# Induced attention and an ELU feed-forward layer on one core: the first batch's product of h and w_in written in place, and a new order of the work

## The chip, the cores and the metric

The kernel runs on one core of a Trainium2 chip. The metric is the device time of one execution in microseconds (us). A core has five engines that run side by side, each through its own list of instructions in order: TensorE (PE, matmuls), VectorE (DVE), ScalarE (ACT), GpSimd (POOL) and SyncE (SP), which here issues all the transfers. They wait for one another by semaphores only. PE writes to PSUM, which DVE and ACT read and POOL cannot.

## What is computed

The reference, cut to what matters (B = 4, N = 12480, C = 128, m = 32 inducing rows, d_ff = 2048):

```python
def mab(q, kv):
    s = scale * (q @ kv.transpose(0, 2, 1))
    s = s - s.max(-1, keepdims=True)
    a = np.exp(s)
    a /= a.sum(-1, keepdims=True) + 1e-09
    return a @ kv
h = mab(I, x)              # [B, 32, 128]
x = mab(x, h)              # [B, N, 128]
h = x @ w_in               # [B*N, 2048]
g = np.where(h > 0.0, h, alpha * (np.exp(np.minimum(h, 0.0)) - 1.0))
return (g @ w_out).astype(np.float32)
```

The weights w_in and w_out come as float64, the rest as float32.

## The kernel before

**Work.** Each batch of 12480 rows is cut into 25 blocks of 512 or 480 rows, in seven groups of 4, 4, 4, 3, 4, 4 and 2 blocks. A batch goes through two halves. The first half gives h of the batch: per group, scores against the inducing rows (`scores`, L443; PE tile ps_s, then a copy s on ACT and a row maximum pm on DVE), a common bias from the maxima so far (`bias_of`, L466), exp on ACT and a transpose eT on DVE (`weights_of`, L502), and the weighted sum of x (`gather`, L515; PE tile ps_hh). At the end the sums es are added up (`sum_es`, L547), h is normalised (`norm_h`) and transposed four times side by side into hT4 (`spread_h`, L583, tile hT). The second half is the attention of x to h (`attend`, L630; scores ps_t, softmax on DVE, ACT and POOL, tiles s2, mx, sm and aT) and the two layers.

**Product of h and w_in.** Instead of the attention output times w_in the kernel multiplies the 32 attention weights of a row by the 32 x 2048 product h @ w_in. Both factors are split into a high and a low float32r part, so layer one is a product of a stack of 96 rows (high, high, low of the attention weights, the tiles stk, and rows of 1/32 below) with a stack hw of 96 rows (high, low, high of the product, and rows of 1 below). `project_h` (L593) makes hw: four matmuls beside one another, each 32 rows wide, put a quarter of the product into each quarter of the partitions of one PSUM tile ps_hw; ACT copies the high part, DVE subtracts to get the low part, and 12 transfers of 64 KB move the pieces to their rows and columns of hw (L620).

**Layers.** A unit (`unit`, L722) is 256 of the 2048 columns for one block: two layer-one matmuls into a PSUM buffer ph (three of these), exp on ACT (e), a max/min step on DVE, the split of the result into gh and gl, and layer-two matmuls into po (L796). Eight units make a block. The plan "PDPDPDPN" says for each which engine makes gl: POOL (P, L765 and L769), DVE (D, L760), or none, with a slower fp32 matmul instead (N).

**First batch.** Its x arrives in row layout (tiles xm), is transposed by PE (ps_x, L866) and copied to xT by DVE and ACT in turn (L875). For the other batches x arrives a second time as xq and DVE transposes it (L419). The first half of batch 1 is spread over the units of batch 0. The first block of batch 0 has an attention of its own (`attend` with lone), all on DVE and ACT, which writes its stk directly.

**Weights.** Each 512-column piece of a float64 weight goes through `weight_steps` (L355): nine steps on DVE, ACT and POOL that put the double together as a float32. There are four pieces of w_in and four of w_out; w_out is then split into wo_h (ACT, L918) and wo_l (POOL, L921), 128 columns at a time.

**Order.** All instructions are first collected as operations with an engine, a key, an estimated duration and what they read and write. `Program.order` (L134) then simulates them: on each engine it takes, of the operations that could start at the earliest time or within LOOK ns of it, the one with the smallest key. It assumes a wake-up time for an operation that waits for another engine (WAKE), a hold of 60 ns for each transfer on SP, a half-speed PE up to 40 us (WARM), and gives out two PSUM banks for all that isn't ph: ps_s, ps_hh, ps_t, ps_hw and po share them. The result is one fixed list per engine. Buffers of one tag are reused in program order. All durations in it are the planner's own estimates.

Of the kernel before, what the change touches and what calls it, by code (L numbers as in the profile page):

```python
# [17 lines left out]
P = 128  # L18
Q = 32
# [59 lines left out]
class Program:  # L79
# [167 lines left out]
def pe(n, passes=1):  # L247
    return passes * n / 2.4 + (17 if passes == 1 else 5), 165.0
# [3 lines left out]
def kernel(  # L252
# [102 lines left out]
    def weight_steps(raw, lo, key, dst, last):  # L355
        part = new([P, WS], U32, "o", "w_part")
        n = WS

        def words():
# [29 lines left out]
        add("DVE", key, dve(n)[0], lambda: nc.vector.scalar_tensor_tensor(  # L389
            out=words()[0].bitcast(F32), in0=words()[1], scalar=2.0**-20,  # L390
            in1=words()[0].bitcast(F32), op0=ALU.mult, op1=ALU.add,
        ), r=[H, L], w=[L], lag=108)
# [4 lines left out]
    def load_raw(t, src, key):  # L397
        add("SP", key, 60.0, src, w=[(t, "d")], nbytes=4 * math.prod(t.shape))
# [8 lines left out]
    def load_xT(b, h, key):  # L407
# [5 lines left out]
        for dq in range(4):  # L413
            add("SP", key, 60.0, lambda dq=dq: nc.sync.dma_start(
                xq()[dq * Q : (dq + 1) * Q],
                src[:, dq * Q : (dq + 1) * Q].rearrange("(u t) d -> t u d", t=Q),
            ), r=[("w_out",)], w=[(xq, dq)], nbytes=n * Q * 4 * 2)
# [24 lines left out]
    def scores(b, g, key):  # L442
# [15 lines left out]
        add("ACT", key, act(T, True)[0], lambda: nc.scalar.copy(  # L458
# [32 lines left out]
    def load_xm(b, g, v, key, tag="xm"):  # L491
# [10 lines left out]
    def weights_of(b, g, i, key):  # L502
# [8 lines left out]
        add("DVE", key, dve(T, True)[0], lambda: nc.vector.transpose(e()[:np_], s()[:np_]),  # L511
# [3 lines left out]
    def gather(b, g, key, first, scale):  # L515
# [17 lines left out]
        if first:  # L533
            h = st["h"] = new([P, C], F32, "h", f"h_{b}")
            add("DVE", key, dve(C)[0], lambda: nc.vector.tensor_copy(h(), ps()[:, :C]),
                r=[(ps, 0)], w=[(h, 0)], lag=108)
        elif scale is not None:
            h = st["h"]
            add("DVE", key, dve(C)[0], lambda: nc.vector.scalar_tensor_tensor(
                out=h(), in0=h(), scalar=scale(), in1=ps()[:, :C], op0=ALU.mult, op1=ALU.add  # L540
            ), r=[(ps, 0), (h, 0), (scale, 0)], w=[(h, 0)], lag=108)
# [51 lines left out]
    def project_h(b, key):  # L593
# [23 lines left out]
        for c in range(4):  # L617
            for i in range(3):
                part = (hw_h, hw_l)[i % 2]
                add("SP", key, 60.0, lambda c=c, i=i, part=part: nc.sync.dma_start(  # L620
                    hw()[i * Q : (i + 1) * Q, c * n : (c + 1) * n].bitcast(F32),
                    part()[c * Q : (c + 1) * Q, :].bitcast(F32),
                ), r=[(part, 0)], w=[(hw, c, i)], nbytes=Q * n * 4)

# [97 lines left out]
    def unit(b, k, cp):  # L722
# [19 lines left out]
        add("PE", n, 2 * pe(T)[0], layer_one,  # L742
# [3 lines left out]
        add("ACT", n, act(2 * T, True)[0], lambda: nc.scalar.activation(  # L746
# [3 lines left out]
        add("DVE", n + KMID, dve(2 * T)[0], lambda: nc.vector.scalar_tensor_tensor(  # L750
            out=ga(), in0=ph()[:, :, :T], scalar=1.0, in1=e(), op0=ALU.max, op1=ALU.min
        ), r=[(ph, 0), (e, 0)], w=[(g, 0)], lag=108)
        if how != "N":
            gh = new(shape, F32R, "gh", f"gh_{n}")
            add("ACT", n + KGH[how], act(2 * T, how == "D")[0], lambda: nc.scalar.activation(  # L755
# [3 lines left out]
        if how == "D":  # L759
            add("DVE", n + KGL, dve(2 * T)[0], lambda: nc.vector.scalar_tensor_tensor(  # L760
# [3 lines left out]
        else:  # L764
            add("POOL", n + KMID, pool_one(2 * T)[0], lambda: nc.gpsimd.tensor_scalar(  # L765
                out=e(), in0=e(), scalar1=-1.0, scalar2=1.0, op0=ALU.add, op1=ALU.mult
            ), r=[(e, 0)], w=[(e, 0)], lag=45)
        if how == "P":
            add("POOL", n + KMID, pool_two(2 * T)[0], lambda: nc.gpsimd.tensor_sub(  # L769
# [18 lines left out]
        for m, piece in enumerate(pieces):  # L788
# [14 lines left out]
            add("PE", n + KOUT, len(piece) * one, layer_two,  # L803
                r=reads + [("wo", 2 * cp), ("wo", 2 * cp + 1)], w=[(po, cp, m)], lag=165)
        if cp == NCP - 1:
            o = new([P, U, Q], F32, "o", f"o_{b}_{k}")
# [5 lines left out]
            for dq in range(4):  # L812
                add("SP", n + KOUT, 60.0, lambda dq=dq: nc.sync.dma_start(
# [202 lines left out]
```

## Time and profile before

| | |
|---|---|
| time, median of 3 runs | 1746.35 us (1746.22 to 1750.83) |
| profiled execution | 1745.76 us, of it the span from first to last instruction 1744.0 us |
| mean granted PE clock | 0.981 of full |
| moved by DMA | 98.18 MB, mean 56 GB/s |
| DVE / ACT / POOL busy | 1530.7 / 1487.9 / 1564.5 us |

All times inside the profile count from the first instruction. A busy time of an engine is the sum of its instructions; matmuls overlap, and their durations contain the pipeline. "Idle before" is the time an engine stood before an instruction, and the arrow names what ended it. L is a line of the kernel; SPq is the queue of transfers on SP. In the tables a group of instructions is one line with the count behind x, the busy time in us and the mean in ns. In the list by time the first column is the start in us, the second the length. The granted clock is the share of PE's pulses that the chip let through in a stretch.

### The profile page before, as it was taken

How to read it: one execution, taken by the hardware profiler on the slowest of the kernel's cores; microseconds unless marked ns; L12 is line 12 of the kernel's file. 1: busy time of each engine (PE TensorE's matmuls, PEld its weight loads, DVE VectorE, ACT ScalarE, POOL GpSimd, SP SyncE). 2: the span in 40 equal slices, each digit the busy share in tenths (PEclk: the TensorE clock that was granted, in tenths of full speed). 3: DMA queues.
4: the chain of work that ended last, by engine and by line, in shares of the span. 5: the costliest groups of instructions: out<-in, count | busy, mean ns of one | idle time of the engine just before them, and what ended most of it. 6: DMA issues, size and time to landing. Idle time of an engine off the chain costs nothing.

```text
span 1744.0 us, 23334 instructions
## 1 busy us (share of the span) xinstructions
PE 1667.7 (96%) x7652; PEld 1198.6 (69%) x7652; DVE 1530.7 (88%) x1610; ACT 1487.9 (85%) x1710; POOL 1564.5 (90%) x1041
## 2 busy tenths in 40 slices
PE   5679999999999999999999999999999999999998
PEld 3357766767766776677766776667776777777776
DVE  5789889898899989988899989998889989888886
ACT  5479989888888988888988988889888889989986
POOL 3479999999898999799999999989999999999998
PEclk8689999999999999999999999999999999999999
DMA  8341232232333233222144223112112111111111
GB/s 268 68 73 40 52 80 57 52 83 51 74 73 66 55 71 73 56 64 52 40 78 71 51 57 68 26 45 52 38 36 45 26 31 29 26 31 31 27 18 18
DMA packets 384762, 98.18 MB, mean 56 GB/s; under 512 B 364864, under 2 KB 370784, under 8 KB 384384
## 3 DMA queue, kind: packets, MB, share of 16 engines
q1 hardware_dynamic: 384640, 96.68, 26.0%
q8 instruction: 61, 1.00, 0.2%
q14 instruction: 61, 0.50, 0.1%
HBM read 48.94 MB, written 25.56 MB: 43 GB/s over the span
## 4 chain that ended last, share of the span: by engine, by line
PE 63%; POOL 13%; DVE 11%; issue 6%; ACT 5%; DMA 2%; SPq 0%; POOLq 0%; DVEq 0%; ACTq 0%
PE po L796 45%; PE ph L736 15%; POOL gl L769 7%; POOL e L765 4%; DVE e L750 3%; ACT e L746 2%; DVE gl L760 2%; DVE ph L750 2%; ACT gh L755 2%; PE ps_t_False L645 1%; PE ps_s L451 1%; POOL alo L705 1%; PE ps_hh L523 1%; DVE apart L471 1%; DVE sm_False L679 1%
## 5 line engine op out<-in xcount | busy, mean ns | idle before, releaser
L769 POOL TENSOR_TENSOR gl<-e,gh 128x1024 fp32r<-128x1024 f32 (+1 forms) x400 | 940.0, 2351 | 19.5
L746 ACT ACTIVATE e<-ph 128x1024 f32<-128x1024 f32 (+1 forms) x800 | 782.9, 1007 | 121.1 <-PE ph L736 112.6
L750 DVE SCALAR_TENSOR_TENSOR e<-ph,e 128x1024 f32<-128x1024 f32 (+1 forms) x500 | 590.8, 1187 | 122.9 <-ACT e L746 118.6
L765 POOL TENSOR_SCALAR e<-e 128x1024 f32<-128x1024 f32 (+1 forms) x500 | 511.9, 1031 | 100.2 <-ACT gh L755 87.0
L796 PE MATMUL po<-gh,wo_h 128*128 128x512 f32 (+1 forms) x1400 | 557.1, 398 | 3.7 <-DVE o L807 2.0
L796 PE MATMUL po<-gh,wo_l 128*128 128x512 f32 (+1 forms) x1400 | 546.1, 390 | 0.0
L736 PE MATMUL ph<-stk,hw 128*128 128x512 f32 (+1 forms) x1600 | 488.9, 405 | 25.2 <-DVE e L750 16.3
L755 ACT ACTIVATE gh<-e 128x1024 fp32r<-128x1024 f32 (+1 forms) x400 | 417.9, 1045 | 39.1 <-DVE e L750 35.9
L796 PE MATMUL po<-gl,wo_h 128*128 128x512 f32 (+1 forms) x1400 | 444.0, 410 | 5.9 <-POOL gl L769 5.6
L736 PEld LDWEIGHTS ph<-stk,hw 128*128 128x128 f32 x1600 | 292.6, 189 | 143.1 <-DVE e L750 33.4
L760 DVE SCALAR_TENSOR_TENSOR gl<-ph,gh 128x1024 fp32r<-128x1024 f32 (+1 forms) x300 | 356.3, 1188 | 35.3 <-ACT gh L755 34.4
L750 DVE SCALAR_TENSOR_TENSOR ph<-ph,e 128x1024 f32<-128x1024 f32 (+1 forms) x300 | 357.0, 1190 | 3.3 <-ACT e L746 2.9
L796 PEld LDWEIGHTS po<-gl,wo_h 128*128 128x128 f32 x1400 | 253.4, 188 | 118.4 <-POOL gl L769 55.3
L755 ACT ACTIVATE gh<-ph 128x1024 fp32r<-128x1024 f32 (+1 forms) x300 | 301.5, 1005 | 31.8 <-DVE ph L750 20.7
L796 PEld LDWEIGHTS po<-gh,wo_h 128*128 128x128 f32 x1400 | 263.7, 188 | 85.8 <-ACT gh L755 14.7
L796 PEld LDWEIGHTS po<-gh,wo_l 128*128 128x128 f32 x1400 | 263.6, 188 | 54.1 <-issue 3.3
L796 PE MATMUL po<-e,wo_n 128*128 128x512 f32 (+1 forms) x400 | 187.5, 591 | 0.5 <-POOL e L765 0.5
L796 PEld LDWEIGHTS po<-e,wo_n 128*128 128x128 f32 x400 | 75.7, 192 | 58.6 <-issue 48.6
L807 DVE STREAM_TRANSPOSE o<-po 128x512 f32<-128x512 f32 (+1 forms) x100 | 69.2, 692 | 11.5 <-PE po L796 11.2
L419 DVE STREAM_TRANSPOSE xT<-xq 128x1024 f32<-128x1024 f32 (+2 forms) x39 | 45.0, 1155 | 5.2 <-DMA xq<-in_x_dram 5.0
L451 PE MATMUL ps_s<-xT,indT 128*32 128x512 f32 (+1 forms) x200 | 33.0, 642 | 16.8 <-DVE xT L875 10.7
L669 POOL TENSOR_TENSOR s_False<-s_False,mx_False 128x512 f32<-128x512 f32 (+3 forms) x28 | 28.9, 1032 | 15.3 <-DVE mx_False L666 15.3
(98 smaller groups left out, 572.4 us busy)
## 6 DMA issues: line engine op xcount, KB each, us to landing
xm<-in_x_dram SPq DMA_DIRECT2D x32, 512.0 KB, 4.5
out_dram<-o SPq DMA_DIRECT2D x240, 64.0 KB, 1.9
xq<-in_x_dram SPq DMA_DIRECT2D x84, 128.0 KB, 3.0
out_dram<-o SPq DMA_DIRECT2D x160, 60.0 KB, 1.9
stk<-ahi SPq DMA_DIRECT2D x118, 64.0 KB, 2.0
xq<-in_x_dram SPq DMA_DIRECT2D x60, 120.0 KB, 2.9
stk<-ahi SPq DMA_DIRECT2D x80, 60.0 KB, 2.0
stk<-alo SPq DMA_DIRECT2D x59, 64.0 KB, 2.0
```

The costliest lines, as they stand in the source:

```text
L419: add("DVE", key + 4.0, dve(n, True)[0], lambda: nc.vector.transpose(t(), xq().rearrange("p u d -> p (u d)")), r=[(xq, dq) for dq in range ...
L451: nc.tensor.matmul(ps()[j * Q : (j + 1) * Q, :T], indT, block_xT(b, g0 + j), start=True, stop=True)
L669: add(on, at(), two[0], lambda: eng.tensor_tensor(out=s(), in0=s(), in1=mx()[:np_].unsqueeze(2).broadcast_to([np_, U, Q]), op=ALU.subtract ...
L736: nc.tensor.matmul(ph()[:, j, :T], st["hw"]()[:, f * P : (f + 1) * P], homes[i][:, :T], start=True, stop=True,)
L746: add("ACT", n, act(2 * T, True)[0], lambda: nc.scalar.activation(e(), ph()[:, :, :T], AF.Exp, bias=-1.0), r=[(ph, 0)], w=[(e, 0)], lag=118)
L750: add("DVE", n + KMID, dve(2 * T)[0], lambda: nc.vector.scalar_tensor_tensor(out=ga(), in0=ph()[:, :, :T], scalar=1.0, in1=e(), op0=ALU.ma ...
L755: add("ACT", n + KGH[how], act(2 * T, how == "D")[0], lambda: nc.scalar.activation(gh(), ga(), AF.Copy, bias=-1.0), r=[(g, 0)], w=[(gh, 0) ...
L760: add("DVE", n + KGL, dve(2 * T)[0], lambda: nc.vector.scalar_tensor_tensor(out=gl(), in0=ga(), scalar=-1.0, in1=gh().bitcast(F32), op0=AL ...
L765: add("POOL", n + KMID, pool_one(2 * T)[0], lambda: nc.gpsimd.tensor_scalar(out=e(), in0=e(), scalar1=-1.0, scalar2=1.0, op0=ALU.add, op1= ...
L769: add("POOL", n + KMID, pool_two(2 * T)[0], lambda: nc.gpsimd.tensor_sub(gl(), e(), gh().bitcast(F32)), r=[(e, 0), (gh, 0)], w=[(gl, 0)], ...
L796: nc.tensor.matmul(po()[:, :T], w(), g_(), start=po.count == 0, stop=po.count == po.total - 1)
L807: add("DVE", n + KOUT - 1, dve(T, True)[0], lambda: nc.vector.transpose(o().rearrange("p u d -> p (u d)"), po()[:, :T]), r=po.parts, w=[(o ...
```

## The change

It has four parts.

1. A new `project_first` makes hw of batch 0 (the other batches keep `project_h`). hT4 holds h four times side by side, so one matmul with all of it gives the product in all four quarters of the partitions: for each quarter of the columns one full-width fp32 matmul into a ph buffer, an ACT copy of 96 rows into hw, and a DVE subtraction that replaces rows 32 to 63 by the low part. No transfer is left in it. The transfers of batch 1 (xq) wait until the last PE operation of `project_first` has run.
2. Batch 0 uses two softmax phases (groups 0 to 2 and 3 to 6) instead of five.
3. w_out is split in steps of up to 512 columns instead of 128: three whole quarters, and a quarter in two pieces of 256. One piece of w_in and one of w_out (WALT) do one DVE step on ACT and POOL instead. The temporary of w_out's pieces uses the buffers of xq instead of those of o.
4. The planner's estimates, look-aheads and all keys are new: a transfer holds SP for 590 ns, PE's wake-up is 200 ns and 60 more for who waits for PE, no slow start of PE, and each kind of operation has its own key offset. In the first stage the attention chain of batch 0 has smaller keys than all steps of the weights.

The core of the diff:

```diff
-WARM = 40000.0
-KMID, KGL, KOUT = 1.0, 1.6, 5.0
-KGH = {"D": 1.5, "P": 2.0}
-KATT = (-37.6, 2.2)
-KWIN, KWOUT, KWSTEP = -1000.0, -20.0, 4.0
-LOADS = (-1009.0, -1008.0, -1007.0, -1006.0)
+WARM = 0.0
+ISSUE = 590.0
+LOOK0 = 0.0
+KATT = (-44.1, 3.68)
-LOOKS = {"PE": 0.0, "ACT": 60.0, "DVE": 60.0, "POOL": 0.0, "SP": 0.0}
+LOOKS = {'PE': 191, 'ACT': 149, 'DVE': 243, 'POOL': 0.0, 'SP': 0.0}
+
+K = {'inP': 0.28, 'inD': -1.6, 'inN': -2.15, 'expP': 1.04, 'expD': 0.24, 'expN': 1.15, 'midP': 1.28, 'midD': 0.66, 'midN': -1.32, 'ghP': 2.33, 'ghD': 1.92, 'glD': -1.13, 'oneP': -0.51, 'oneN': 1.03, 'glP': -1.63, 'outP': 5.59, 'outD': 5.97, 'outN': 6.56, 'late': 0.86, 'o': 5.08}
+KP = {'g': 1.0, 'px': 1.34, 'cx': -5.03, 'ps': -3.68, 's': -1.1, 'pm': -0.4, 'bias': 8.29, 'exp': -3.31, 'eT': -3.94, 'hh': 5.83, 'h': -6.1, 'es': 2.17, 'end': -5.15, 'hw': -0.01, 'win': 30.77, 'winstep': 16.36, 'wout': 20.28, 'woutstep': 0.66, 'in0': -9.2, 'in1': 14.96, 'out': 22.66, 'outstep': 2.93, 'hwlate': 0.0}
+PHASES0 = [range(0, 3), range(3, 7)]
+WALT = [0, 0, 0, 1, 0, 0, 0, 1]
...
-    WAKE = {"PE": 60.0, "ACT": 35.0, "DVE": 35.0, "POOL": 90.0, "SP": 60.0}
+    WAKE = {"PE": 200.0, "ACT": 35.0, "DVE": 35.0, "POOL": 90.0, "SP": 60.0}
...
+    def wake(self, of, by):
+        return 5.0 if of == by else self.WAKE[by] + 60.0 * (of == "PE")
...
-                    if op.at is not None and op.at <= base + self.LOOK[e]:
+                    look = self.FIRST if op.key < -950.0 else self.LOOK[e]
+                    if op.at is not None and op.at <= base + look:
...
-        add("DVE", key, dve(n)[0], lambda: nc.vector.scalar_tensor_tensor(
-            out=words()[0].bitcast(F32), in0=words()[1], scalar=2.0**-20,
-            in1=words()[0].bitcast(F32), op0=ALU.mult, op1=ALU.add,
-        ), r=[H, L], w=[L], lag=108)
+        if alt:
+            add("ACT", key, act(n)[0], lambda: nc.scalar.activation(
+                words()[1].bitcast(F32), words()[1], AF.Copy, scale=2.0**-20
+            ), r=[H], w=[H], lag=118)
+            add("POOL", key, pool_two(n)[0], lambda: nc.gpsimd.tensor_tensor(
+                out=words()[0].bitcast(F32), in0=words()[1].bitcast(F32), in1=words()[0].bitcast(F32),
+                op=ALU.add,
+            ), r=[H, L], w=[L], lag=50)
...
-            ), r=[("w_out",)], w=[(xq, dq)], nbytes=n * Q * 4 * 2)
+            ), r=[("w_out",), ("begun",)], w=[(xq, dq)], nbytes=n * Q * 4 * 2)
...
+    def project_first(key, late):
+
+        st = get(0)
+        n = F // 4
+        hw = st["hw"] = new([P, F], F32R, "hw", "hw_0")
+        add("POOL", key - 20, 1760.0, lambda: nc.gpsimd.memset(hw()[3 * Q :, :].bitcast(F32), 1.0),
+            w=[(hw, "one")], lag=45)
+        for c in range(4):
+            ps = new([P, 2, 512], F32, "ph", f"ps_hw_{c}")
+            add("PE", key + c * late, pe(n, 4)[0], lambda c=c, ps=ps: nc.tensor.matmul(
+                ps()[:, 0, :n], st["hT4"](), win_sb[:, c * n : (c + 1) * n], start=True, stop=True
+            ), r=[(st["hT4"], 0), ("win", c)], w=[(ps, 0)], lag=165)
+
+            def part(i, m, c=c):
+                return hw()[i * Q : (i + m) * Q, c * n : (c + 1) * n]
+
+            add("ACT", key + c * late, act(n, True)[0], lambda ps=ps, part=part: nc.scalar.copy(
+                part(0, 3), ps()[: 3 * Q, 0, :n]
+            ), r=[(ps, 0)], w=[(hw, c, i) for i in range(3)], lag=118)
+            add("DVE", key + c * late, dve(n)[0], lambda ps=ps, part=part: nc.vector.tensor_sub(
+                part(1, 1), ps()[Q : 2 * Q, 0, :n], part(1, 1).bitcast(F32)
+            ), r=[(ps, 0)], w=[(hw, c, 1)], lag=108)
...
-    PHASES0 = [range(0, 2), range(2, 4), range(4, 5), range(5, 6), range(6, 7)]
...
-    project_h(0, CH + 8)
+    project_first(at("hw"), KP["hwlate"])
+
+    prog.writer[("begun",)] = [o for o in prog.ops if o.eng == "PE"][-1]
...
-        for j in range(n):
-            f = quarter * n + j
...
+        for lo, m in ([(0, n)] if all(f in WHERE_S for f in fs) else [(0, 2), (2, 2)]):
+            f = quarter * n + lo
...
-                add("ACT", key + 0.1 * j, act(C)[0], lambda w=w, piece=piece: nc.scalar.copy(
-                    wo_h[:, w, :], piece()), r=[done], w=[("woh", f)], lag=118)
+                add("ACT", key, act(m * C)[0], lambda w=w, lo=lo, m=m, piece=piece: nc.scalar.copy(
+                    home_of(wo_h, w, m), piece(lo, m)
+                ), r=[done], w=[("woh", f)], lag=118)
```

More of the change, by code (lines that the diff above doesn't have):

```diff
@@ L222, in order @@
                     o.ready,
-                    op.start if o.before[op] else op.end + (self.WAKE[o.eng] if o.eng != op.eng else 5.0),
+                    op.start if o.before[op] else op.end + self.wake(op.eng, o.eng),
                 )
@@ L247, in pe @@
 def pe(n, passes=1):
-    return passes * n / 2.4 + (17 if passes == 1 else 5), 165.0
+    return passes * n / 2.4 + (20 if passes == 1 else 8), 165.0
 @with_exitstack
@@ L353, in words_of, with weight_steps @@
         return r[:, :, 0], r[:, :, 1]
-    def weight_steps(raw, lo, key, dst, last):
-        part = new([P, WS], U32, "o", "w_part")
+    def weight_steps(raw, lo, key, dst, last, tag, alt):
+        part = new([P, WS], U32, tag, "w_part")
         n = WS
@@ L510, in weights_of, with gather @@
         e = new([P, T], F32, "eT", f"eT_{b}_{g}")
-        add("DVE", key, dve(T, True)[0], lambda: nc.vector.transpose(e()[:np_], s()[:np_]),
+        add("DVE", key_e, dve(T, True)[0], lambda: nc.vector.transpose(e()[:np_], s()[:np_]),
             r=[(s, 0)], w=[(e, 0)], lag=108)
         st["e", g] = e
-    def gather(b, g, key, first, scale):
+    def gather(b, g, key, first, scale, key_h=None):
+        key_h = key if key_h is None else key_h
         st = get(b)
@@ L745, in unit @@
             w=[(ph, 0)], lag=165)
-        add("ACT", n, act(2 * T, True)[0], lambda: nc.scalar.activation(
+        add("ACT", n + K["exp" + how], act(2 * T, True)[0], lambda: nc.scalar.activation(
             e(), ph()[:, :, :T], AF.Exp, bias=-1.0
@@ L764, in unit @@
         else:
-            add("POOL", n + KMID, pool_one(2 * T)[0], lambda: nc.gpsimd.tensor_scalar(
+            add("POOL", n + K["one" + how], pool_one(2 * T)[0], lambda: nc.gpsimd.tensor_scalar(
                 out=e(), in0=e(), scalar1=-1.0, scalar2=1.0, op0=ALU.add, op1=ALU.mult
@@ L884 @@
             transpose_first(g)
-            scores(0, g, CH + g)
-        bias_of(0, i, groups.stop, CH + groups.stop - 1)
+            scores(0, g, at("ps", g), at("s", g), at("pm", g))
+        bias_of(0, i, groups.stop, at("bias", groups.stop - 1))
         for g in groups:
-            weights_of(0, g, i, CH + g)
-            gather(0, g, CH + g, g == 0, get(0)["scale", i] if i and g == groups.start else None)
-    sum_es(0, PHASES0, CH + 7)
-    share_of(0, CH + 7)
-    norm_h(0, CH + 7)
-    spread_h(0, CH + 7)
-    attend(0, 0, CH + 8, 0.0, lone=True)
-    project_h(0, CH + 8)
+            weights_of(0, g, i, at("exp", g), at("eT", g))
+            gather(0, g, at("hh", g), g == 0, get(0)["scale", i] if i and g == groups.start else None,
+                   at("h", g))
+    sum_es(0, PHASES0, at("es"))
+    share_of(0, at("es"))
+    norm_h(0, at("end"))
+    spread_h(0, at("end"))
+    attend(0, 0, at("end"), 0.0, lone=True)
+    project_first(at("hw"), KP["hwlate"])
+    prog.writer[("begun",)] = [o for o in prog.ops if o.eng == "PE"][-1]
     for quarter in range(4):
@@ L913 @@
+        fs = range(quarter * n, (quarter + 1) * n)
+        for lo, m in ([(0, n)] if all(f in WHERE_S for f in fs) else [(0, 2), (2, 2)]):
+            f = quarter * n + lo
             if f in WHERE_N:
-                add("ACT", key + 0.1 * j, act(C)[0], lambda f=f, piece=piece: nc.scalar.copy(
-                    wo_n[:, WHERE_N[f], :], piece()), r=[done], w=[("wo", f)], lag=118)
+                add("ACT", key, act(m * C)[0], lambda w=WHERE_N[f], lo=lo, m=m, piece=piece: nc.scalar.copy(
+                    home_of(wo_n, w, m), piece(lo, m)
+                ), r=[done], w=[("wo", f + j) for j in range(m)], lag=118)
@@ L926, in first_half @@
+                add("POOL", key, pool_two(m * C)[0] + 100, lambda w=w, lo=lo, m=m, piece=piece:
+                    nc.gpsimd.tensor_sub(
+                        home_of(wo_l, w, m), piece(lo, m), home_of(wo_h, w, m).bitcast(F32)
+                    ), r=[done, ("woh", f)], w=[("wo", f + j) for j in range(m)], lag=50)
     def first_half(b):
```

99 lines of the change are left out of this document (55 added, 44 removed).

## The prediction

> **What bounds the kernel now.** I read the page first (busy shares and the 40 slices), then the busy time of each engine in chosen stretches, then the instructions in order of time up to 125 us, then the waits and the groups of single engines in that part.
>
> ```profile
> PE 1667.7 (96%) x7652; PEld 1198.6 (69%) x7652; DVE 1530.7 (88%) x1610; ACT 1487.9 (85%) x1710; POOL 1564.5 (90%) x1041
> ...
> PE   5679999999999999999999999999999999999998
> ```
>
> PE is the bound over the whole run, but the first three slices of 43.6 us read 5, 6 and 7. So two different stages have to be priced: a start-up in which PE is half idle, and a long stage in which it hardly ever is. Busy time by stretch shows the border (columns: length, then PE, PEld, DVE, ACT, POOL with their counts, granted PE clock, DMA share, GB/s):
>
> ```profile
> 0.00:10.00 10.00, 2.28 (x11) 2.18 (x12) 2.61 (x10) 4.95 (x7) 4.61 (x20) 1.00 0.77 270
> 10.00:20.00 10.00, 7.94 (x58) 5.47 (x57) 8.15 (x14) 3.32 (x6) 5.60 (x5) 1.00 1.03 364
> 20.00:30.00 10.00, 7.09 (x106) 4.95 (x104) 4.74 (x12) 5.55 (x12) 0.00 (x0) 1.00 1.04 329
> ...
> 140.00:150.00 10.00, 10.00 (x42) 7.52 (x42) 9.03 (x11) 9.03 (x11) 9.92 (x6) 1.00 0.31 64
> ...
> 40.00:60.00 20.00, 12.77 (x146) 9.10 (x142) 17.16 (x39) 13.57 (x33) 10.77 (x14) 0.76 0.27 56
> ...
> 0.00:83.40 83.40, 47.73 (x424) 27.96 (x424) 55.00 (x112) 37.67 (x82) 34.75 (x54) 0.77 0.58 169
> 83.40:102.60 19.20, 10.13 (x28) 4.53 (x25) 14.76 (x17) 12.77 (x15) 9.67 (x7) 0.59 0.71 114
> 102.60:107.20 4.60, 4.58 (x11) 3.65 (x12) 3.83 (x4) 1.58 (x3) 1.27 (x2) 0.53 0.44 108
> 107.20:1744.00 1636.80, 1605.30 (x7194) 1162.45 (x7192) 1457.08 (x1478) 1435.87 (x1612) 1518.78 (x980) 1.00 0.24 50
> ```
>
> From 107.2 us on PE is idle for 1636.8 - 1605.3 = 31.5 us in all, at full clock. A better order can win no more than that there. Before 83.4 us PE runs only the first batch's attention; DVE, its busiest helper, works 55.0 of 83.4 us, 66%, though from 40 to 60 us it reaches 17.16 of 20, 86%. The loads keep the DMA engines full only to about 30 us: 2.70 + 3.64 + 3.29 = 9.6 MB have moved by then. What is left up to 83 us is waiting in an order that does not fit:
>
> ```profile
> DVE w_part L378 <- POOL w_part L374: 6.9, 4, 3.0
> ...
> PE ps_s L451 <- DVE xT L875: 10.7, 4, 8.2
> ```
>
> DVE stands 6.9 us behind POOL in the weight conversion (us, times, longest), and PE stands up to 8.2 us at once for copies of xT that DVE holds back. The end of the start-up, in order of time:
>
> ```profile
> 55.09 1.00 PE L451 MATMUL ps_s<-xT,indT 128*32 128x480 f32 x4 [1.35 <-DVE h L539]
> ...
> 69.90 0.29 DVE L590 COPY hT<-ps_ht 128x128 f32<-128x128 f32 x1 [1.32 <-PE ps_ht L587]
> 70.25 2.08 PE L645 MATMUL ps_t_True<-xT,hT 128*128 128x512 f32 x2 [0.38 <-DVE hT L590]
> 72.25 1.94 PE L600 MATMUL ps_hw<-win_sb,hT 128*32 128x512 f32 x8
> 74.94 5.01 SPq L620 DMA_DIRECT2D hw<-hw_h  x8
> 75.92 1.25 DVE L419 STREAM_TRANSPOSE xT<-xq 128x1024 f32<-128x1024 f32 x1 [0.27 <-PE ps_t_False L645]
> 77.08 0.64 DVE L675 TENSOR_REDUCE sm_True<-s_True 128x16 f32<-128x512 f32 x1
> 77.65 1.23 DVE L419 STREAM_TRANSPOSE xT<-xq 128x1024 f32<-128x1024 f32 x1
> 80.06 2.43 SPq L620 DMA_DIRECT2D hw<-hw_l  x4
> 81.47 0.68 DVE L697 TENSOR_TENSOR stk<-aT_True,stk 32x512 fp32r<-32x512 f32 x1
> 83.45 2.92 PE L736 MATMUL ph<-stk,hw 128*128 128x512 f32 x6
> 86.31 1.12 PE L645 MATMUL ps_t_False<-xT,hT 128*32 128x512 f32 x8
> 101.78 0.69 DVE L660 STREAM_TRANSPOSE s_False<-ps_t_False 128x512 f32<-128x512 f32 x1
> 102.62 0.76 PE L796 MATMUL po<-gh,wo_h 128*128 128x512 f32 x1 [0.62 <-DVE s_False L660]
> ```
>
> The first layer-one matmul starts at 83.45 us, 13.3 us after hT is there (70.2). The first layer-two matmul comes only at 102.62: it waits for the PSUM bank that DVE empties at 101.78, though those scores were written at 86.3 to 87.4.
>
> I reduce this to two terms. t1 is the first layer-one matmul, 83.45. The loss after t1 is what PE misses from there to 107.2: of 23.75 us it did 16 layer-one and 11 layer-two matmuls, worth 0.238 us each at full rate (42 in 10 us), 6.4 us, and eight score matmuls, 1.12 us at about half clock, say 0.5. So 23.75 - 6.9 = 16.8 us are lost. PE could as well have begun at full rate at 83.45 + 16.8 = 100.2 us.
>
> **The change part by part.**
>
> *Product of h and the first weight.* Out go the eight narrow matmuls (1.94 us), one copy, one subtraction and 12 transfers, which hold SP from 74.94 to 82.49. In come four full-width fp32 matmuls, four copies on ACT and four subtractions on DVE, all into hw itself. On the path the transfers cost 83.45 - 82.15 (the end of the subtraction into stk) = 1.3 us, and no more: until then stk is the later one. The new matmul has the shape of ps_t_True, so four take 4 x 2.08 = 8.3 us at the clock granted there and lie beside DVE's chain for the first block. That chain took 82.15 - 69.9 - 0.3 = 12 us from hT; without the two transposes of xq inside it (75.92 and 77.65, 2.5 us) and with the two extra waits gone I take about 9, between 8 and 11.
>
> The clock decides whether PE is late instead. The stretch 83.4 to 102.6 has 0.59, the next 0.53, and a 4-pass matmul at the full clock is
>
> ```profile
> 116.33 1.88 PE L796 MATMUL po<-e,wo_n 128*128 128x512 f32 x4
> ```
>
> 0.94 us. If the four stay slow, hw is complete 2.1 + 8.3 = 10.4 us after hT; layer one would then start 1.4 us after stk. If they speed up, hw is early. I keep 9 and put the 1.4 us into the range. The Trainium skill, "TensorE: Matmul & The Clock Gate", Part 1, says that about 3.4 us of sustained work release the full clock; by it the four would be done after about 7.4 us and cost nothing. In the trace the granted clock is full right after 4.6 us of dense work (102.6 to 107.2), which agrees.
>
> *Transfers of the second batch held back* until the first batch's product is issued on PE. The cost on DVE and the place of the transfers on SP:
>
> ```profile
> 26.16 12.83 SPq L414 DMA_DIRECT2D xq<-in_x_dram  x8
> ...
> L419 DVE STREAM_TRANSPOSE xT<-xq 128x1024 f32<-128x1024 f32 x3 | 3.7, 1236 | 0.3 <-PE ps_t_False L645 0.3
> L559 DVE SCALAR_TENSOR_TENSOR es<-es,scale,es 128x1 f32<-128x1 f32 x4 | 2.6, 641 | 0.0
> L389 DVE SCALAR_TENSOR_TENSOR w_out<-w_out 128x512 f32<-128x512 uint32 x4 | 3.0, 750 | 0.0
> L471 DVE TENSOR_TENSOR apart<-pm,mine 128x8 f32<-128x8 f32 (+4 forms) x5 | 1.5, 298 | 0.1
> L611 DVE TENSOR_TENSOR hw_l<-ps_hw,hw_h 128x512 fp32r<-128x512 f32 x1 | 0.7, 691 | 0.4 <-ACT hw_h L609 0.4
> ...
> L393 POOL TENSOR_TENSOR w_out<-w_out,w_part 128x512 f32<-128x512 f32 x4 | 6.2, 1548 | 5.6 <-DVE es L559 5.5
> L921 POOL TENSOR_TENSOR wo_l<-w_out,wo_h 128x128 fp32r<-128x128 f32 x14 | 8.7, 648 | 1.2 <-ACT wo_h L918 1.2
> ```
>
> Eight transfers of 128 KB leave the window in which w_in and w_out still arrive, and 3.7 us leave DVE before t1. They come back in the first batch's 400 us, where DVE has slack (1457.1 of 1636.8 us busy); if that cover is gone they cost at most their 3.7 us.
>
> *Two softmax phases instead of five.* Three phases fewer take from DVE 3 x (0.64 + 0.30 + about 0.3 for the two small reductions) = 3.7 us, and three serial steps pm, bias, exp. The price: the first gathers wait for the third group's scores, so the buffers for w_out come free a little later. w_out is needed only at the first layer-two matmul, which has slack.
>
> *Weights.* Two of eight 512-column pieces move one DVE step (0.75) to ACT and POOL: DVE -1.5 us. The subtractions of w_out on POOL go from fourteen of 0.65 to three of 512 columns (1.55 by L393) and one of half that: 8.7 to about 5.5 us. Both lie off the path if the order is right, so I count only DVE's part.
>
> *Replanned order.* DVE's work up to t1 becomes 55.0 - 3.7 - 3.7 - 1.5 + 3 x 0.69 = 48.2 us. At the old share of 66% that takes 73 us; at the 86% of the stretch 40 to 60, with the first 10 us and their 2.6 us as they are, 10 + 45.6 / 0.86 = 63 us. A lower end comes from the data: w_in (2.1 MB) and the first batch of x (6.4 MB), which go ahead of all else, are in by about 27 us at the rates above. From the last group's scores to hT it is 70.2 - 55.1 = 15 us; with about 1 us of transposes and copies ahead of them and 9 from hT to layer one, 52. The new priorities put the attention chain ahead of the weights on every engine, so I take 62 for t1, between 52 and 73.
>
> The loss after t1 cannot fall to nothing. From the first layer-one pair to the first layer-two matmul stand these steps:
>
> ```profile
> 89.58 1.21 DVE L750 SCALAR_TENSOR_TENSOR e<-ph,e 128x1024 f32<-128x1024 f32 x1
> 90.82 1.06 ACT L755 ACTIVATE gh<-e 128x1024 fp32r<-128x1024 f32 x1 [3.26 <-DVE e L750]
> 100.37 1.02 ACT L746 ACTIVATE e<-ph 128x1024 f32<-128x1024 f32 x1
> ```
>
> 0.97 (a pair in the row at 83.45) + 1.02 + 1.21 + 1.06 = 4.3 us, less three layer-one pairs done meanwhile (1.4), plus 2.3 for a slow clock over 4.6 us: 5.2 us. The other end is today's 16.8. I take 10, near the middle, since the bank wait may return in part.
>
> In the long stage I take 6 of the 31.5 us of idle time as won, between 0 and 16; the order there changes everywhere, and no row shows how well it fits. Sum, against the profiled execution's 1745.76 us (span 1744.0 and 1.76 around it): t1 -21.5, loss -6.8, long stage -6: 1711.5. The median of the runs is 0.6 us above that execution, so 1712.
>
> **The rivals.** *The gain is handed back after t1* (faster, but little). Layer one starts early, but layer two still waits for a bank or the last of w_out. For: PE stood 19 us between the two at 83.45 and 102.62 and the two banks stay. Against: DVE's work before is smaller. If the first layer-two matmul comes at 92 instead of 102.6, that is all there is: 1746.4 - 10.6 = 1736.
>
> *The chain up to hT does not move*, the weights' arrival sets it. Then only the transfers (1.3) and the transposes inside the last chain (2.5) are won: 1742.5, within the noise. Against it: the DMA share falls to 0.27 after 40 us, 30 us ahead of hT.
>
> *The new order costs PE in the long stage*, and the kernel is slower. POOL is the place:
>
> ```profile
> L769 POOL TENSOR_TENSOR gl<-e,gh 128x1024 fp32r<-128x1024 f32 (+1 forms) x400 | 940.0, 2351 | 19.5
> ```
>
> 400 units need this 2.35 us step and POOL is busy 1518.8 of 1636.8 us, 0.3 us of slack for each. If the new order brings each one late enough that PE stands 0.1 us for it, that is 40 us: 1745.8 - 28.3 + 40 = 1757.5. It decides from 28.3 / 400 = 0.07 us each. Against: POOL's own work is not increased there, and PE's present waits are small.
>
> **How the numbers follow.** My forecast 0.72, handed back 0.13, chain unmoved 0.05, slower 0.07; 0.03 for less than 1694. A measurement of this kernel can tell about 0.3%, 5.2 us. Faster: 0.72 + 0.13 + 0.03 = 0.88; same 0.05; slower 0.07. The ends of the forecast are not reached all at once; t1 52 to 73, loss 5.2 to 16.8 and 0 to 16 us combine to about 1694 to 1733, and with half of the first rival the range is 1694 to 1735.
>
> **What would show it.** In the profile of the changed kernel: the first ph matmul near 62 us, no stk or hw transfer before it, no L419-like transpose ahead of it; hT near 53; the first po matmul within 6 us of the first ph; PE full from about 72 on; idle time of PE after that near 25 us. A t1 above 73, a po that waits for a bank, or over 45 us of idle PE afterwards would prove me wrong, each in its own step.

## The result, and the profile after

The changed kernel takes 1698.88 us (median of 4 runs, 1697.87 to 1699.32) against 1746.74 before: a ratio of 0.972, 95% interval 0.9703 to 0.9737, or 48 us less. The profiled execution took 1697.87 us, 1696.1 of it span. The page of the changed kernel, busy shares and slices:

```profile
PE 1651.0 (97%) x7646; PEld 1199.3 (71%) x7646; DVE 1526.8 (90%) x1599; ACT 1485.5 (88%) x1701; POOL 1562.9 (92%) x1033
...
PE   6799999999999999999999999999999999999998
```

At the start two slices instead of three lie below 9. The amounts of work on DVE, ACT and POOL are nearly those of before; what changed is when it is done. The same kernel, busy time by stretch, cut at the first layer-one matmul, the first layer-two matmul and just ahead of full rate:

```profile
0.00:69.10 69.10, 44.62 (x418) 26.65 (x418) 52.10 (x99) 38.45 (x73) 33.97 (x46) 0.83 0.59 185
69.10:78.80 9.70, 6.55 (x16) 3.33 (x12) 8.73 (x12) 8.96 (x11) 4.68 (x4) 0.50 0.35 55
78.80:83.20 4.40, 4.32 (x10) 3.47 (x11) 4.40 (x4) 2.66 (x3) 4.40 (x4) 0.51 0.43 104
83.20:1696.10 1612.90, 1595.51 (x7207) 1165.82 (x7205) 1461.53 (x1487) 1435.48 (x1615) 1519.89 (x982) 1.00 0.25 52
```

The full clock begins at 83.2 us, not at 107.2: 24.0 us are won by then. The long stage behind it takes 1612.9 us, not 1636.8: another 23.9. So the gain has two halves of about one size, and I had forecast the first at 28 and the second at 6.

The end of the start-up in the changed kernel, in order of time, PE and DVE:

```profile
54.51 0.28 DVE L612 COPY hT<-ps_ht 128x128 f32<-128x128 f32 x1
54.72 2.50 DVE L391 TENSOR_SCALAR w_out<-w_out 128x512 uint32<-128x512 uint32 x2
54.85 2.08 PE L690 MATMUL ps_t_True<-xT,hT 128*128 128x512 f32 x2 [0.66 <-DVE hT L612]
56.72 4.00 PE L656 MATMUL ps_hw<-win_sb,hT 128*128 128x512 f32 x6
57.73 0.70 DVE L705 STREAM_TRANSPOSE s_True<-ps_t_True 128x512 f32<-128x512 f32 x1
61.64 1.13 PE L656 MATMUL ps_hw<-win_sb,hT 128*128 128x512 f32 x2
66.43 0.71 DVE L705 STREAM_TRANSPOSE s_False<-ps_t_False 96x512 f32<-96x512 f32 x1
67.29 1.93 PE L690 MATMUL ps_t_False<-xT,hT 128*32 128x512 f32 x8 [3.53 <-DVE s_False L705]
67.89 0.68 DVE L742 TENSOR_TENSOR stk<-aT_True,stk 32x512 fp32r<-32x512 f32 x1
69.15 2.93 PE L781 MATMUL ph<-stk,hw 128*128 128x512 f32 x6
78.88 0.77 PE L841 MATMUL po<-gh,wo_h 128*128 128x512 f32 x1 [1.22 <-DVE s_False L705]
```

hT is there at 54.8 us (before 70.2), but the first layer-one matmul comes 14.3 us after it, later than the 13.3 of before. Weight steps stand in front of the chain (from 54.72), and the next group's softmax (from 66.43) in front of its last step. The wait for a bank ahead of the first layer-two matmul is there again, at 78.88 instead of 102.62.

In the long stage of the kernel before, the two stretches around its longest waits; then two of about the same part of the work in the changed kernel:

```profile
705.00:745.00 40.00, 35.64 (x161) 23.91 (x160) 36.92 (x36) 32.25 (x42) 31.01 (x21) 0.96 0.19 48
1110.00:1150.00 40.00, 36.45 (x140) 25.64 (x139) 36.08 (x36) 30.62 (x34) 33.30 (x23) 0.96 0.12 23
```

```profile
640.00:700.00 60.00, 59.96 (x276) 42.95 (x274) 54.30 (x54) 54.64 (x60) 58.23 (x37) 1.00 0.25 52
1050.00:1110.00 60.00, 59.97 (x275) 42.80 (x274) 54.06 (x54) 54.16 (x60) 59.14 (x38) 1.00 0.25 50
```

Before, PE was idle for 4.4 and 3.6 us there, with 0.96 of its clock; after, for next to nothing, at full clock. The waits of PE in the long stage (us, times, longest), before and after:

```profile
PE ph L736 <- DVE e L750: 8.8, 6, 3.5
PE ph L736 <- DVE gl L760: 7.2, 12, 1.6
PE po L796 <- POOL gl L769: 5.6, 22, 0.5
```

```profile
PE ph L781 <- DVE e L795: 4.9, 7, 1.7
PE po L841 <- DVE o L852: 2.6, 3, 1.1
PE po L841 <- POOL gl L814: 1.4, 5, 0.5
PE ph L781 <- DVE gl L805: 0.6, 3, 0.2
```

Layer one waited 16.0 us for DVE (e and gl) and now waits 5.5; layer two waited 5.6 us for gl from POOL and now 1.4.

### The profile page after: what moved, and what is told of

It reads as the page before. It is cut to its first block, busy times and chain, and to the rows that moved or that the text cites. A ratio compares the mean times of both kernels' runs of the same rounds, so it can differ in the third digit from the quotient of the medians.

```text
span 1696.1 us, 23562 instructions
## 1 busy us (share of the span) xinstructions
PE 1651.0 (97%) x7646; PEld 1199.3 (71%) x7646; DVE 1526.8 (90%) x1599; ACT 1485.5 (88%) x1701; POOL 1562.9 (92%) x1033
## 4 chain that ended last, share of the span: by engine, by line
PE 73%; POOL 13%; DVE 5%; issue 4%; ACT 4%; DMA 1%; POOLq 0%; SPq 0%; DVEq 0%; ACTq 0%
PE po L841 52%; PE ph L781 17%; POOL gl L814 7%; POOL e L810 5%; ACT gh L800 2%; ACT e L791 2%; PE ps_t_False L690 1%; PE ps_s L471 1%; DVE e L795 1%; PE ps_hh L545 1%; DVE ph L795 1%; DVE gl L805 0%; POOL s_False L730 0%; DMA xm<-in_x_dram 0%; DVE xT L925 0%
## 5 line engine op out<-in xcount | busy, mean ns | idle before, releaser
L791 ACT ACTIVATE e<-ph 128x1024 f32<-128x1024 f32 (+1 forms) x800 | 775.3, 1007 | 84.6 <-PE ph L781 80.9
L781 PE MATMUL ph<-stk,hw 128*128 128x512 f32 (+1 forms) x1600 | 480.5, 407 | 8.1 <-DVE e L795 6.9
L841 PE MATMUL po<-gl,wo_h 128*128 128x512 f32 (+1 forms) x1400 | 437.0, 404 | 2.3 <-POOL gl L814 1.4
L545 PE MATMUL ps_hh<-xm,eT 128*32 128x128 f32 (+2 forms) x872 | 33.6, 295 | 7.0 <-DVE eT L532 4.2
L545 PEld LDWEIGHTS ps_hh<-xm,eT 128*32 128x32 f32 (+2 forms) x872 | 25.2, 117 | 16.6 <-issue 11.3
```

Of the source, the lines that this page charges most:

```text
L545: nc.tensor.matmul(ps()[c * Q : (c + 1) * Q, :C], st["e", g]()[:np_, u * Q : (u + 1) * Q], st["xm", g, u - u % UP]()[:np_, u % UP, :], sta ...
L781: nc.tensor.matmul(ph()[:, j, :T], st["hw"]()[:, f * P : (f + 1) * P], homes[i][:, :T], start=True, stop=True,)
L791: add("ACT", n + K["exp" + how], act(2 * T, True)[0], lambda: nc.scalar.activation(e(), ph()[:, :, :T], AF.Exp, bias=-1.0), r=[(ph, 0)], w ...
L841: nc.tensor.matmul(po()[:, :T], w(), g_(), start=po.count == 0, stop=po.count == po.total - 1)
```

## The experiments

My theory after the result: the start-up and the long stage were each made about 24 us shorter, independently. The rival for the long stage: it is shorter because the start-up hands it another state. For the start-up: the order (attention chain ahead of the weights) against the amount of work, the new product, or the planner's estimates. Each kernel ran in three rounds beside the kernel before, whose median was 1746.7 to 1750.8 us on the chips used; so ratios are compared, and 0.001 is 1.75 us. "Full rate" is the start of the first single layer-two matmul of about 0.4 us in the list by time of the profiled execution, and "rest" is what follows it up to the end of the span.

| kernel | hT | first layer one | first layer two | full rate | rest | ratio (95%) |
|---|---|---|---|---|---|---|
| before | 70.2 | 83.5 | 102.6 | 107.5 | 1636.5 | 1 |
| changed | 54.8 | 69.2 | 78.9 | 84.2 | 1611.9 | 0.9720 (0.9703 to 0.9737) |
| e9 old planner, long stage | 53.5 | 69.0 | 78.9 | 84.3 | 1638.7 | 0.9859 (0.9843 to 0.9875) |
| e2 old keys, long stage | 53.6 | 66.7 | 77.5 | 80.6 | 1670.9 | 1.0005 (0.9996 to 1.0015) |
| e5 old estimates, long stage | 54.6 | 70.1 | 80.9 | 86.9 | 1616.9 | 0.9757 (0.9739 to 0.9775) |
| e6 before, new product | 70.5 | 84.6 | 100.4 | 104.3 | 1638.3 | 0.9994 (0.9982 to 1.0005) |
| e1 old product | 54.7 | 68.6 | 83.9 | 89.5 | 1613.6 | 0.9737 (0.9717 to 0.9757) |
| e3 five phases | 56.8 | 70.6 | 80.4 | 84.3 | 1615.0 | 0.9731 (0.9710 to 0.9751) |
| e7 no hold | 54.6 | 68.3 | 78.0 | 83.5 | 1611.5 | 0.9712 (0.9689 to 0.9734) |
| c2 planned with a slow PE | 60.3 | 70.5 | 75.3 | 75.6 | 1623.1 | 0.9726 (0.9706 to 0.9745) |
| c1 look-ahead of 250 ns | 50.2 | 72.3 | 87.1 | 91.8 | 1612.8 | 0.9748 (0.9734 to 0.9763) |
| s1 old keys, start-up | 59.2 | 73.6 | 83.3 | 88.7 | 1611.8 | 0.9715 (0.9697 to 0.9734) |
| s3 old keys and estimates, start-up | 66.1 | 78.3 | 89.6 | 93.5 | 1615.8 | 0.9777 (0.9761 to 0.9794) |
| e10 no DVE step on ACT and POOL | 55.8 | 71.3 | 81.0 | 86.5 | 1611.7 | 0.9704 (0.9689 to 0.9718) |

The rest is 1611.5 to 1616.9 us with the new keys in the long stage, but for c2, and 1636.5 to 1638.7 with the old keys and old estimates, whatever the start-up before it took. So, but for c2, what the start-up gains or loses is carried to the end of the span to within 4 us.

**The long stage with the planner of before (e9).** Operations of the long stage get the old keys, look-aheads, wake-ups and costs; the start-up stays new.

```diff
-KATT = (-44.1, 3.68)
+KATT = (-37.6, 2.2)
-LOOKS = {'PE': 191, 'ACT': 149, 'DVE': 243, 'POOL': 0.0, 'SP': 0.0}
+LOOKS = {"PE": 0.0, "ACT": 60.0, "DVE": 60.0, "POOL": 0.0, "SP": 0.0}
+K = {'inP': 0, 'inD': 0, 'inN': 0, 'expP': 0, 'expD': 0, 'expN': 0, 'midP': 1.0, 'midD': 1.0, 'midN': 1.0, 'ghP': 2.0, 'ghD': 1.5, 'glD': 1.6, 'oneP': 1.0, 'oneN': 1.0, 'glP': 1.0, 'outP': 5.0, 'outD': 5.0, 'outN': 5.0, 'late': 0.0, 'o': 4.0}
+        if key > -900.0:
+            return 5.0 if of == by else self.OLDWAKE[by]
+    if STAGE[0]:
+        return 0.828 * n + (54 if psum else 69), 118.0
```

> The changed kernel, but for the operations of the long stage the planner has the keys, look-aheads and estimates of before; the start-up is that of the changed kernel. Theory (the gain has two halves of about 24 us, the start-up and the planner's order in the long stage): the second half is lost, 1718 to 1728 us, with PE idle over 28 us after the start-up. Rival (the long stage got shorter because the start-up hands it another state): 1698 to 1705 us.

1723.77 us: 0.0139 in the ratio, 24 us, are lost, though the start-up ends at the same time. The stretch from its full rate to the end of the span at 1723.0, and its waits of PE there:

```profile
84.50:1760.00 1675.50, 1608.92 (x7202) 1161.81 (x7200) 1462.78 (x1486) 1437.10 (x1615) 1520.56 (x980) 1.00 0.24 50
```

```profile
PE ph L797 <- DVE e L811: 9.0, 6, 3.5
PE ph L797 <- DVE gl L821: 7.7, 14, 1.6
PE po L857 <- POOL gl L830: 4.8, 19, 0.4
```

PE is idle for 1723.0 - 84.5 - 1608.9 = 29.6 us, and the waits are those of the kernel before nearly to the number. With the new start-up in front the old planner has its old long stage back, so the rival falls.

**Keys or estimates in the long stage (e2, e5).** e2 takes only the old K, KATT and LOOKS of the diff above; e5 only the old wake-ups, costs and 60 ns for a transfer.

> The changed kernel with the keys and look-aheads of before in the long stage; the planner's estimates stay new. Theory A (the keys and look-aheads make the order of the long stage): 1714 to 1728 us. Theory B (the estimates make it): 1697 to 1705 us.

> The changed kernel with the planner's estimates of before (wake-up times, costs of the engines, 60 ns for a transfer) in the long stage; keys and look-aheads stay new. Theory A (keys and look-aheads): 1697 to 1706 us. Theory B (estimates): 1714 to 1728 us.

Old keys with new estimates lose everything, 50 us in the ratio, twice what the old planner as a whole loses. In e2, from full rate to the end at 1751.5, and its waits:

```profile
80.50:1760.00 1679.50, 1619.94 (x7210) 1165.78 (x7209) 1465.58 (x1487) 1436.75 (x1616) 1523.12 (x982) 1.00 0.24 50
```

```profile
PE ph L781 <- DVE gl L805: 14.9, 24, 2.7
PE po L841 <- POOL gl L814: 9.9, 27, 1.1
PE ph L781 <- DVE e L795: 5.7, 5, 2.5
```

PE is idle for 51.1 us, with the waits for gl doubled. New keys with old estimates lose 0.0037, some 6 us, and their full rate alone comes 2.7 us later (86.9). So the new keys carry the long stage under either set of estimates, and it is the old keys that lose more under the new ones. Theory A was right in direction and far too low for e2: it took keys and estimates to add up, and they don't.

**The new product alone (e6), and all but the new product (e1).**

```diff
-    project_h(0, CH + 8)
+    project_first(CH + 8, 0.0)
```

> The kernel before with nothing but the product of h and w_in of the first batch made in place. Theory (the transfers were 1.3 us on the path, the rest lay beside other work): 1741 to 1747 us, and the first layer-one matmul between 81 and 84 us. Rival (the new product is a main part of the start-up's gain): under 1737 us, first layer-one matmul before 79 us.

```diff
-    project_first(at("hw"), KP["hwlate"])
+    project_h(0, at("hw"))
```

> The changed kernel with the old product for the first batch (eight narrow matmuls and 12 transfers into hw), planned anew. Theory (the transfers lie beside the first block's attention, which took 14.3 us from hT to the first layer-one matmul in the changed kernel): 1698 to 1703 us, first layer-one matmul at most 3 us later than 69.15. Rival (the new product carries the start-up's gain once the rest is in order): 1706 us or more.

In the old order the product brings nothing that can be measured, and layer one does not start earlier; 1747.26 us and 84.6 lie just above the theory's 1747 and 84, and far from the rival. In the new order taking it out costs 0.0017, within the intervals of both, but the full rate comes 5.4 us later, so a few us are not excluded. Two lines of e1:

```profile
68.64 2.93 PE L781 MATMUL ph<-stk,hw 128*128 128x512 f32 x6
83.94 0.77 PE L841 MATMUL po<-gh,wo_h 128*128 128x512 f32 x1 [0.62 <-DVE s_False L705]
```

With its 12 transfers layer one begins 0.5 us earlier than without; what is late is layer two, by 5 us, behind the bank again. Whether the transfers or only another plan make it late is not shown.

**Phases (e3).** PHASES0 with the five ranges of before.

> The changed kernel with five softmax phases in the first batch instead of two. Theory (3.7 us of DVE work and three serial chains more, not the main part): 1700 to 1707 us, hT 2 to 6 us later than 54.8. Rival (the phases were what held the start-up): 1712 us or more.

hT comes 2.0 us later, the least that was expected, and the ratio rises by 0.0011, not beyond its interval. The rival falls.

**The hold (e7).**

```diff
-            ), r=[("w_out",), ("begun",)], w=[(xq, dq)], nbytes=n * Q * 4 * 2)
+            ), r=[("w_out",)], w=[(xq, dq)], nbytes=n * Q * 4 * 2)
```

> The changed kernel without the hold on the second batch's transfers, which may start once w_out is on its way. Theory (3.7 us of DVE work and 1 MB of transfers in the start-up): 1699 to 1705 us. Rival (the hold is what let the weights in early): 1708 us or more.

Nothing that can be measured changes (1698.51 us, just under the theory's range), and the theory's 1 MB never moved: without the hold the first transfers of batch 1 still start at the same time. The queue in e7, then in the changed kernel:

```profile
60.17 10.98 SPq L432 DMA_DIRECT2D xq<-in_x_dram  x12
```

```profile
60.36 11.69 SPq L432 DMA_DIRECT2D xq<-in_x_dram  x12
```

The temporaries of w_out now lie in the two buffers of xq, which come free only when w_out's pieces are done with them. So it is not the hold that keeps these transfers back; the buffers, by the code, are what is left.

**Order or amount in the start-up (c2, c1).** c2 lets the planner believe in a half-speed PE between 33 and 80 us; c1 sets LOOK0 to 250.

```diff
-            if op.eng == "PE" and start < self.warm:
+            if op.eng == "PE" and 33000.0 < start < 80000.0:
```

> The changed kernel, planned with a PE at half speed between 33 and 80 us, as the granted clock shows it. Theory (from hT to the first layer-one matmul DVE took 13.9 us instead of 9 since the plan puts weight steps ahead of the chain where it believes PE done earlier): first layer-one matmul 2 to 5 us earlier, 1693 to 1698 us. Rival (DVE's amount of work sets that point, not its order): 1697 to 1702 us.

> The changed kernel with a look-ahead of 250 ns in the start-up, so that an engine waits a moment for the attention chain rather than begin a weight step. If order still loses time in the start-up: first layer-one matmul 2 to 4 us earlier than 69.15, 1694 to 1698 us. If the amount of work on DVE sets that point: 1697 to 1703 us.

In c2 the way from hT to layer one takes 10.1 us instead of 14.3, near what I had forecast for the change itself:

```profile
60.04 0.29 DVE L612 COPY hT<-ps_ht 128x128 f32<-128x128 f32 x1 [1.32 <-PE ps_ht L609]
70.45 2.90 PE L781 MATMUL ph<-stk,hw 128*128 128x512 f32 x6 [2.74 <-DVE stk L742]
75.27 0.50 PE L841 MATMUL po<-gh,wo_h 128*128 128x512 f32 x1
```

But hT is 5.5 us later, and layer one 1.3 us later than in the changed kernel, as the rival has it: the weight steps that no longer stand behind hT stand before it. c2 has its full rate 8.6 us ahead of the changed kernel and is no faster, 0.9726. Each from its full clock on to 120 us, c2 and then the changed kernel:

```profile
75.60:120.00 44.40, 39.56 (x162) 25.10 (x161) 44.30 (x47) 38.31 (x43) 40.32 (x27) 1.00 0.50 90
83.20:120.00 36.80, 36.38 (x155) 25.85 (x154) 34.81 (x37) 32.19 (x36) 33.47 (x23) 1.00 0.48 87
```

In c2 DVE is busy for 44.30 of 44.40 us there, and PE stands for 4.8 us, 3.7 of them for DVE, against 0.4 in the changed kernel. Of the 7.6 us of lead 4.4 go this way; another 3.1 were none, since c2 had 9 layer matmuls behind it and the changed kernel 22. So DVE's work was put off, not saved.

In c1 hT is 4.6 us earlier and layer one 3.1 us later, and the time, 1706.77 us, lies above both ranges. Two of its lines:

```profile
59.41 0.68 DVE L742 TENSOR_TENSOR stk<-aT_True,stk 32x512 fp32r<-32x512 f32 x1
71.17 2.07 PE L656 MATMUL ps_hw<-win_sb,hT 128*128 128x512 f32 x2 [4.11 <-POOL win_sb L411]
```

Here stk is done at 60.1 us, 9.9 us after hT, so the length that I had forecast is there even with an early hT. Layer one waits for the last piece of w_in, which POOL finishes at 71.1 us. Its last steps on DVE and POOL stand behind steps of w_out, which is needed only by layer two; the keys say so too (20.28 for w_out, 30.77 and more for w_in). DVE meanwhile stands idle for 7.0 us, from 65.8 to 72.8. So c1 is late by the order of the weights, not by DVE's amount of work. An order with all of w_in ahead of w_out was not tried.

**Keys and estimates in the start-up (s1, s3).** s1 gives the steps of a group nearly one key, w_in's pieces keys beside the first groups, w_out's behind the first units; s3 adds the old estimates for operations with keys up to -900.

```diff
+KP = {'g': 1.0, 'px': 0.0, 'cx': 0.0, 'ps': 0.0, 's': 0.0, 'pm': 0.5, 'bias': 0.0, 'exp': 0.0, 'eT': 0.0, 'hh': 0.0, 'h': 0.0, 'es': 7.0, 'end': 7.0, 'hw': 8.0, 'win': 0.0, 'winstep': 0.512, 'wout': 980.0, 'woutstep': 4.0, 'in0': -9.2, 'in1': 14.96, 'out': 22.66, 'outstep': 2.93, 'hwlate': 0.0}
```

> The changed kernel with the start-up's keys as before: all steps of a group share one key, w_in's pieces stand beside the first groups and w_out behind the first units. Theory (most of the start-up's gain is the attention chain going ahead of the weights): hT 6 to 14 us later than 54.8, 1706 to 1716 us. Rival (the planner's estimates make the start-up's gain, the keys do little): 1697 to 1703 us.

> As the run with the start-up's old keys, and with the planner's estimates of before in the start-up too (60 ns for a transfer, short wake-ups, a slow PE up to 40 us); new product and two phases stay. Theory (keys first, estimates second): 1708 to 1722 us, at most 5 us above the run with the old keys alone. Rival (estimates first): over 8 us above that run.

My theory falls here. The keys delay hT by 4.4 us only, and the ratio is that of the changed kernel. In the profiled executions they do cost their part: the full rate comes 4.5 us later and the span is 4.4 us longer, 1700.5; the ratio does not show it, as the kernel before took 4 us more on this chip. The old estimates cost 9.9 us more on the same chip (1711.88 against 1702.03) and bring hT to 66.1. So of the 23.3 us by which the full rate comes earlier than in the kernel before, taken in this order, the estimates make 4.8 and the keys 4.5; the other 14.0 are in what s3 keeps, the new work and buffers and a look-ahead of 0 in the start-up, and were not separated. DVE's waits up to 69.1 us in s3, then in the changed kernel:

```profile
DVE w_part L389 <- DMA w_in<-in_moe_w_in_dram: 6.7, 2, 3.9
DVE w_part L403 <- POOL w_part L399: 5.9, 3, 2.7
```

```profile
DVE w_part L373 <- DMA w_in<-in_moe_w_in_dram: 2.6, 1, 2.6
DVE w_part L387 <- POOL w_part L383: 2.3, 4, 0.9
```

With a transfer counted at 60 ns, and the other old estimates, DVE stands 7.7 us longer for w_in and for POOL. Which of the estimates does it was not separated.

**The two moved DVE steps (e10).** WALT all zero.

> The changed kernel without the two pieces that do a DVE step on ACT and POOL. Theory (DVE's amount of work sets the start-up): 1.4 us more on DVE, 1698 to 1701 us. Rival (the two POOL steps cost more than they save, since DVE's steps beside POOL are two to four times as long): 1694 to 1698 us.

DVE was busy for 55.1 us by the first layer one, 3.0 more than in the changed kernel, and layer one and the full rate come 2.1 and 2.3 us later. The ratio is 0.0016 lower, within the intervals, so no effect on the time can be told.

No version was clearly faster than the changed kernel. Not tried either: w_out's smaller steps, its old temporaries, and another order of the first groups' attention.

## Why the prediction held, and where its steps were off

The time lies in the range of the forecast (1712, 1694 to 1735), but this is luck in part: it is the sum of two errors of opposite sign. By one count, which the terms below go through, the start-up won 22.2 us instead of 28.3, and the long stage 25.7 instead of 6, outside its own 0 to 16. The terms:

*hT near 53*: 54.8. The rival in which the chain up to hT does not move is out.

*t1, 62 between 52 and 73*: 69.15, so 14.3 us were won, not 21.5. The step that failed is "I take about 9" from hT to layer one. The two transposes of xq did leave the chain, but weight steps, the next group's softmax and four subtractions into hw took their place. c2 and c1 show about that length, 10.1 and 9.9 us, in plans that keep the chain free; in c2 hT moves the other way, and in c1 the last piece of w_in is late. I put DVE's work up to t1 at 48.2 us; DVE was busy for 52.1 by 69.1, 83% of the time after the first 10 us, close to the 86% that I took. That this work sets t1 is argued, not shown: e10 and e3, with 3.0 and 2.7 us more of it, begin layer one 2.1 and 1.4 us later, but in c1 the order of the weights holds layer one back while DVE stands idle. Of the 3.9 us, 2.9 are weight steps that take longer than before: their groups on DVE sum to 21.5 us, where the 20.1 of before less the two moved steps gives 18.6.

*The transfers, 1.3 us on the path*: e6 finds nothing beyond its interval, which leaves room for some 3 us (0.9982), and in e1 layer one is not late with them. The 1.3 us themselves are too small to be seen.

*The clock of the four new matmuls*: six of their eight halves took 4.00 us, where 8.3 us for all eight at the slow clock would make it 6.2, and hw was done before stk. The four were done at 62.8, 8.0 us after hT, between score matmuls. The 1.4 us were not paid. By the Trainium skill, "TensorE: Matmul & The Clock Gate", Part 1, about 3.4 us of steady work bring the full clock; that the later ones ran fast after some 4 us of work from 54.85 on agrees. But PE then stands 3.53 us for s_False (67.29), and the stretch from 69.1 has 0.50 again.

*The loss after t1, 10 between 5.2 and 16.8*: from 69.15 to 83.2 PE did 12 layer-one and 10 layer-two matmuls, 22 x 0.238 = 5.2 us, of 14.05: the loss is 8.8. The size is right, and the bank wait came back as feared. But the sign that I had set for this step failed: the first layer-two matmul came 9.7 us after the first of layer one, not within 6, and it waited for a bank.

*The long stage, 6 between 0 and 16*: by the same count it went from 1744 - 100.2 = 1643.8 to 1696.1 - 78.0 = 1618.1, 25.7 us. This is the term that was mis-sized most. I had the room, 31.5 us of idle PE, but took a fifth of it, because no row shows how well an order fits. And the room was not the bound that I called it: from the full clock on idle time fell by 14.1 us, to 17.4, and the busy time, which I had taken as fixed, by another 9.8. Of these about 3 are matmuls at a slow clock around the long waits (4% of 40 us, twice). The other 7 are inside the busy time, and what they are stays open. Waits shorter than a matmul's own latency would look so, but that is a guess.

*The hold and the phases*: the transposes left the start-up but for one at 68.6 us, though not by the hold (e7); the phases moved hT by 2.0 us (e3), about half of the 3.7 us of DVE work that I counted.

*The rivals*: the gain was not handed back behind t1, though that rival's mechanism, the bank, is there. The slower long stage did not come, but its danger was real: e2, with nearly the same start-up and other keys, has layer two waiting 9.9 us for POOL's gl and layer one 14.9 for DVE's, and is no faster than before.

## What to carry to other kernels

Where a planner writes the order, a change of its estimates alone can do harm: old keys under new estimates gave 1.0005, both old 0.9859, both new 0.9720, and new keys under old estimates 0.9757. In a start-up that is short of one engine, moving the critical chain about (c1, c2) only changed which part was late; what each stage needs first (here w_in ahead of w_out) and what work can leave that engine are the next things to try, and were not tried here. And price the idle time of a long stage by its whole amount: half of the gain here was 14 us of short waits and what went with them.

## What the runs showed of the hardware

DVE steps on 512 columns took two to four times as long in places. Two of the changed kernel's steps on the tile w_out and the same steps on w_in (minimum, median and maximum in ns), then a long one with the step of POOL beside it:

```profile
L391 DVE TENSOR_SCALAR w_out<-w_out x4: 421/746/1514, 38.7 to 55.7; 128x512 uint32<-128x512 uint32 x4
L407 DVE SCALAR_TENSOR_TENSOR w_out<-w_out x3: 679/1781/1818, 40.3 to 57.1; 128x512 f32<-128x512 uint32 x3
```

```profile
L391 DVE TENSOR_SCALAR w_in<-w_in x4: 398/419/427, 12.7 to 50.4; 128x512 uint32<-128x512 uint32 x4
L407 DVE SCALAR_TENSOR_TENSOR w_in<-w_in x3: 680/682/685, 13.9 to 38.1; 128x512 f32<-128x512 uint32 x3
```

```profile
39.75 1.82 POOL L411 TENSOR_TENSOR win_sb<-w_in,w_part 128x512 f32<-128x512 f32 x1
40.34 1.78 DVE L407 SCALAR_TENSOR_TENSOR w_out<-w_out 128x512 f32<-128x512 uint32 x1
```

The six long weight steps up to 60 us (1.06 to 1.82 us) all began while such a step of POOL with two inputs ran, and ended 0.3 to 0.6 us after it; one that began 0.04 us ahead of such a step (53.91) took its usual 0.69. So part of DVE's busy time there is waiting. The Trainium skill, "SBUF — State Buffer", section "Who interferes with whom", says that VectorE and GpSimd share a pair of ports, held by one instruction to its end while the other blocks. The lengths fit that; no run here separates it by itself.

The second surprise is the price of a pause: around the two longest waits of PE in the kernel before, of 3.5 us each, the granted clock was 0.96 over 40 us, so a pause cost about 1.6 us more than its own length, in matmuls that count as busy. Behind the first of them four matmuls that took 1.88 us at 116.33 take 3.55:

```profile
720.74 0.73 PE L736 MATMUL ph<-stk,hw 128*128 128x512 f32 x2 [3.55 <-DVE e L750]
721.55 3.55 PE L796 MATMUL po<-e,wo_n 128*128 128x512 f32 x4
```
